# A planner that spaces the transfers that are not score shuffles evenly

## The chip, the cores and the metric

The kernel runs on one core of a Trainium2 chip, in one launch. The metric is the device time of that launch in microseconds (us); lower is better. The engines are TensorE (PE in the profile, with its weight loads as PEld), VectorE (DVE), ScalarE (ACT), GpSimd (POOL) and SyncE (SP), which here does nothing but issue DMA transfers. Sixteen DMA engines carry the transfers.

## What is computed

Two stages follow each other: attention whose heads are mixed before and after the softmax, and a feed-forward layer with a rational activation.

```python
B, H, S, D = 4, 12, 448, 64
scores = scale * q @ k.T                                  # (B, H, S, S)
scores = einsum('bhij,hg->bgij', scores, w_pre)           # mix the 12 heads
attn = exp(scores - max) ; attn /= sum(attn) + 1e-9
attn = einsum('bhij,hg->bgij', attn, w_post)              # mix them again
x = (attn @ v) as (B*S, H*D)                              # (1792, 768)
h = x @ w_in                                              # (1792, 2048)
P = a0 + a1*h + a2*h^2 + a3*h^3 ; Q = 1 + |b0|*|h| + |b1|*h^2
out = (P / (Q + 1e-6)) @ w_out                            # (1792, 768)
```

## The kernel before

**Attention** goes through 16 row tiles, T = 0 to 15, four to a batch. A tile has 120 query rows (88 in one tile of each batch). For each of six pairs of heads `put_qk` multiplies q with k on TensorE (line 496), VectorE or ScalarE copies the two score blocks from PSUM to a buffer `st` (lines 238 and 236; there are six such buffers), and one DMA for each head moves the copy into the tile `d` (line 512). This DMA is the **shuffle**: it brings the 12 heads of a row beside each other on the partitions, so that one matmul can mix them. A tile has 12 shuffles, and two tiles `d` are used in turn, so the shuffles of tile T can start only when the last mixing matmul of tile T-2 has read its `d`.

`put_pre` mixes the heads (line 565, `ps_t` or `ps_u` from `d`); its first group of a tile needs all 12 shuffles of that tile. The maximum (571), the exponential (580), the reciprocal (591) and the scaling of the second mixing weights (600) follow, then `put_post` (line 640), a transpose on VectorE (656) and `put_av` (line 705), which multiplies with v. The results go to a scratch tensor in DRAM (`x_scr`, line 728).

**The feed-forward layer** has 64 units: 18 matmuls with `w_in` (line 879), the rational function on ScalarE and VectorE, and 18 matmuls with `w_out` (line 969). The weights are 64-bit in DRAM; `put_w` loads a piece (`cr`, line 405), and ScalarE, VectorE and GpSimd turn it into two 32-bit halves. Three of the 16 blocks of weights are made during attention and stored in a scratch tensor (`w_scr`, line 449).

**The order of everything comes from a planner.** Each step is an `Op` with an engine, an assumed duration, the steps it depends on, an earliest time and a due time `at`. `Plan.run` plays this forward: at each moment it takes the engine that is free first, and of that engine's ready steps the one with the earliest due time. Transfers go through one model of the DMA queue: each `Op` on "sp" adds its `extra` to the time at which the queue is free, and SP may run at most `AHEAD` = 3 us ahead of it. The steps are then written out by their planned start, so each engine's instructions stand in that order. Nothing else of the plan reaches the chip: there every engine takes its own instructions one after the other, each as soon as the semaphores it waits for allow. A transfer that waits for nothing is issued right behind the one before it.

SP's transfers in attention are the shuffles and seven other kinds: q tiles (line 363, `q<-in_q`), pieces of k (375, `kk<-in_k`) and of v (679, `vv<-in_v`), the weight pieces (405, `cr<-in_w`), their stores (449, `w_scr<-co`), the stores of the attention result (728, `x_scr<-xs`), and a few constants. Most of them are made by `bulk`; the weight loads and stores call `add` themselves. `tau[g]` is the planned start of mixing group g, and `END1` the planned start of the feed-forward layer.

Of the kernel before, what the change touches and what calls it, by code (L numbers as in the profile page):

```python
# [37 lines left out]
CV = 384  # L38
# [3 lines left out]


class Op:
    __slots__ = ("eng", "dur", "fn", "deps", "at", "extra", "start", "end", "left", "behind", "since", "n", "on", "pick", "mode", "late")

    def __init__(self, eng, dur, fn, deps, at, extra, since, mode, late):
        self.late = late
        self.since, self.on, self.pick, self.mode = since, None, isinstance(eng, dict), mode
        self.eng, self.dur, self.fn, self.at, self.extra = eng, dur, fn, at, extra  # L50
        self.deps = deps
        self.start = self.end = None


class Plan:
# [6 lines left out]
    SLACK = 2.0  # L62

    def __init__(self):
        self.ops = []

    def add(self, eng, dur, fn, deps=(), at=0.0, extra=0.0, since=0.0, after=(), mode=None, late=0.0):
        op = Op(eng, dur, fn, [d for d in deps if d is not None], at, extra, since, mode, late)
        op.behind = list(after)
        self.ops.append(op)  # L70
        return op

    def run(self):
# [35 lines left out]
                ready(op)  # L109
        order = []  # L110
        last = None
        while True:
            if "sp" in free:
                free["sp"] = max(free["sp"], dma_free - self.AHEAD)
            best = None
            for e in todo:
                while todo[e] and todo[e][0][2].on:
                    heapq.heappop(todo[e])
                while wait[e] and wait[e][0][2].on:
                    heapq.heappop(wait[e])  # L120
                if todo[e]:
                    t = free[e]
                elif wait[e]:
                    t = max(free[e], wait[e][0][0])
                else:
                    continue
                if best is None or t < best[0]:
                    best = (t, e)
# [3 lines left out]
            while wait[e] and wait[e][0][0] <= t:  # L132
                _, n, op = heapq.heappop(wait[e])
                if op.on:
                    continue
                heapq.heappush(todo[e], (op.at, n, op))
            op = todo[e][0][2]
            if e == "pe" and op.mode != last:
                more = [x for x in todo[e] if not x[2].on and x[2].mode == last and x[0] <= op.at + self.SLACK]
                if more:  # L140
                    op = min(more)[2]
# [100 lines left out]
def mixed_attention_then_rational_ffn(ctx: ExitStack, tc, q, k, v, w, wmix, mask, a, b2, out):  # L242
# [8 lines left out]
    plan = Plan()  # L251
# [103 lines left out]

    def bulk(dur, fn, deps, at, nbytes, **more):

        return add("sp", dur, fn, deps, at=at, extra=dma(nbytes), **more)

    def put_q(T, at, since=0.0):  # L360
        def load():
# [37 lines left out]
    def put_w(f, c, at, since=0.0, g=None):  # L399
# [48 lines left out]
        def store():  # L448
            nc.sync.dma_start(out=w_scr[f][:, :, sl], in_=box["o"].bitcast(F32))

        ld = add("sp", 0.45, load, [R["cr"].take()], at=at - 5.0, extra=dma(128 * CV * 8), since=max(since, at - 9.0))
        near = lambda i, k: [] if g is None else [posts[min(g + i, len(groups) - 1)][k]]
        o1 = add("act", act(CV), mag, [ld, R["cm"].take(), *near(0, 3)], at=at, late=4.0)
        o2 = add({"dve": 0.32} if g is None else {"pool": 1.54}, 0, clamp, [o1, *near(0, 1)], at=at)
# [12 lines left out]
        o7 = add(subs(CV, on=ON["w_lo"]), 0, lo, [o6, *near(1, 1)], at=at)  # L467
        R["cm"].uses[-1].append(o7)
        if f in VIA:
            o8 = add("sp", 0.57, store, [o7], at=at, extra=dma(128 * CV * 8), late=2.0)  # L470
            R["co"].uses[-1].append(o8)
            w_done[f].append(o8)
        else:
            w_ld[f].append(o6)
            w_ld[f].append(o7)
# [578 lines left out]
    for u in range(len(units)):  # L1054
# [2 lines left out]
            put_w(i // NCV, i % NCV, at=END1 + UNIT * u + 2.0, since=END1 + UNIT * u - 6.0)  # L1057
        put_unit(u)

    with tc.manual_schedule():  # L1060
        for op in plan.run():
            if op.pick:
                op.fn({"act": nc.scalar, "dve": nc.vector, "pool": nc.gpsimd}[op.on])
            else:
                op.fn()
# [55 lines left out]
```

## Time and profile before

| | |
|---|---|
| time, median of 3 runs | 831.42 us (829.88 to 835.35) |
| the profiled execution: its own time, its span | 830.89 us, 829.1 us |
| TensorE busy | 801.0 us (97%) |
| VectorE, ScalarE, GpSimd busy | 690.6 (83%), 502.4 (61%), 222.2 (27%) |
| moved by DMA | 155.46 MB, 187 GB/s on average |
| TensorE's granted clock | 0.996 of full speed |

The span is the time from the first to the last instruction; 1.8 us of the execution lie around it. A busy TensorE is not a TensorE at its peak, because the ends of matmuls are modelled, so the page says less than the waits do. The granted clock is at its higher level (2.4 GHz) from the first 23 us on.

### The profile page before, as it was taken

The numbers are of one execution on the slowest core, as the hardware profiler recorded it, in microseconds if no ns is written. First come the engines' busy times: TensorE is split into PE (matmuls) and PEld (weight loads), VectorE is DVE, ScalarE is ACT, GpSimd is POOL, SyncE is SP. The second block draws the span as 40 slices with busy tenths as digits, with TensorE's granted clock in tenths as the row PEclk, the third lists the DMA queues.
The fourth block names the chain that finished last, engine by engine and source line by source line (L and its number), as shares of the span: only waits on it lengthen the run. The fifth ranks groups of instructions, "written<-read, shape, count | busy, mean of one in ns | idle before, by whom it ended". The sixth has DMA issues, their size and how long they took to land.

```text
span 829.1 us, 23254 instructions
## 1 busy us (share of the span) xinstructions
PE 801.0 (97%) x9360; PEld 598.0 (72%) x9360; DVE 690.6 (83%) x1252; ACT 502.4 (61%) x1099; POOL 222.2 (27%) x393
## 2 busy tenths in 40 slices
PE   5889999999999999999999999999999999999998
PEld 1244455554554445589999999999999999999997
DVE  5677788887888888888999998999889999677775
ACT  2456666655665566566776775677557677545632
POOL 2224444432444343721111212123212222100000
PEclk9999999999999999999999999999999999999999
DMA  6677878777887675985733255664477634466314
GB/s 201 207 214 224 246 259 265 222 202 231 260 259 212 217 235 171 335 276 210 256 125 101 81 207 133 215 141 104 88 228 192 165 82 67 78 225 231 122 57 156
DMA packets 71900, 155.46 MB, mean 187 GB/s; under 512 B 12560, under 2 KB 52336, under 8 KB 70640
## 3 DMA queue, kind: packets, MB, share of 16 engines
q1 hardware_dynamic: 67736, 141.99, 52.6%
q0 software_dynamic: 3456, 11.01, 8.2%
q8 instruction: 74, 1.21, 0.6%
q10 hardware_dynamic: 600, 0.97, 0.4%
q14 instruction: 34, 0.28, 0.1%
HBM read 77.49 MB, written 37.75 MB: 139 GB/s over the span
## 4 chain that ended last, share of the span: by engine, by line
PE 84%; DMA 6%; DVE 5%; ACT 2%; issue 1%; POOL 0%; SPq 0%; ACTq 0%; DVEq 0%; POOLq 0%
PE ps_s L879 28%; PE ps_u L969 9%; PE ps_t L969 9%; PE ps_a L969 9%; PE ps_s L496 8%; PE ps_a L640 7%; PE ps_t L565 4%; PE ps_u L565 4%; DMA d<-st 4%; PE ps_u L705 2%; PE ps_t L705 2%; DVE nm L571 2%; ACT e L580 2%; DMA kk<-in_k 1%; DVE aa L656 1%
## 5 line engine op out<-in xcount | busy, mean ns | idle before, releaser
L656 DVE STREAM_TRANSPOSE aa<-ps_a 128x448 f32<-128x448 f32 (+1 forms) x184 | 107.8, 618 | 11.6 <-PE ps_a L640 10.8
L879 PE MATMUL ps_s<-d,w 128*128 128x448 f32 x504 | 107.4, 366 | 0.0
L879 PE MATMUL ps_s<-xs,w 128*128 128x448 f32 x504 | 107.1, 366 | 0.0
L236 ACT COPY st<-ps_s 120x448 f32<-120x448 f32 (+1 forms) x120 | 60.4, 533 | 69.2 <-PE ps_s L496 38.3
L496 PE MATMUL ps_s<-kk,q 64*64 64x448 f32 x720 | 94.0, 552 | 8.3 <-DMA kk<-in_k 5.4
L446 POOL TENSOR_TENSOR w<-cm,w 128x384 fp32r<-128x384 f32 x48 | 53.7, 1118 | 177.8 <-ACT w L236 168.4
L600 POOL TENSOR_SCALAR krs<-kpost,rr 128x64 f32<-128x64 f32 x180 | 81.7, 468 | 72.1 <-DVE rr L591 51.3
L879 PEld LDWEIGHTS ps_s<-d,w 128*128 128x128 f32 x504 | 94.3, 188 | 8.7 <-issue 0.9
L879 PEld LDWEIGHTS ps_s<-xs,w 128*128 128x128 f32 x504 | 94.6, 188 | 7.9
L640 PEld LDWEIGHTS ps_a<-e,krs 64*32 64x32 f32 x2880 | 44.7, 106 | 74.4 <-issue 29.0
L640 PE MATMUL ps_a<-e,krs 64*32 64x224 f32 x2880 | 92.6, 355 | 1.6 <-DVE aa L656 0.8
L892 ACT ACTIVATE m<-ps_s,a_sb 128x448 f32<-128x448 f32 x64 | 46.2, 722 | 76.8 <-PE ps_s L879 73.4
L969 PE MATMUL ps_u<-g,w 128*128 128x448 f32 x336 | 84.1, 366 | 0.0
L969 PE MATMUL ps_a<-g,w 128*128 128x448 f32 x336 | 84.1, 366 | 0.0
L969 PE MATMUL ps_t<-g,w 128*128 128x448 f32 x336 | 83.9, 365 | 0.0
L580 ACT ACTIVATE e<-ps_t,nm 128x448 f32<-128x448 f32 x92 | 57.8, 635 | 25.4 <-DVE nm L571 17.1
L580 ACT ACTIVATE e<-ps_u,nm 128x448 f32<-128x448 f32 x88 | 55.3, 635 | 22.0 <-DVE nm L571 18.6
L969 PEld LDWEIGHTS ps_t<-g,w 128*128 128x128 f32 x336 | 63.1, 188 | 5.3
L969 PEld LDWEIGHTS ps_a<-g,w 128*128 128x128 f32 x336 | 63.1, 188 | 5.2
L969 PEld LDWEIGHTS ps_u<-g,w 128*128 128x128 f32 x336 | 63.1, 188 | 5.2
L496 PEld LDWEIGHTS ps_s<-kk,q 64*64 64x64 f32 x720 | 29.5, 135 | 49.4 <-issue 21.5
L915 ACT ACTIVATE ua<-sq 128x448 f32<-128x448 f32 x64 | 37.1, 580 | 33.6 <-DVE sq L912 33.4
(90 smaller groups left out, 1452.7 us busy)
## 6 DMA issues: line engine op xcount, KB each, us to landing
d<-st SPq DMA_DIRECT2D x144, 210.0 KB
cr<-in_w SPq DMA_DIRECT2D x64, 384.0 KB
d<-x_scr SPq DMA_DIRECT2D x5, 2688.0 KB
xs<-x_scr SPq DMA_DIRECT2D x4, 2688.0 KB
o_scr<-o POOLq DMA_DIRECT2D x24, 448.0 KB, 5.7
d<-st SPq DMA_DIRECT2D x42, 157.5 KB
x_scr<-xs SPq DMA_DIRECT2D x12, 540.0 KB
q<-in_q SPq DMA_DIRECT2D x16, 384.0 KB
```

What stands on the lines that cost most here:

```text
L236: eng.copy(o, i)
L446: eng.tensor_sub(t[:, 1, :], box["m"].bitcast(F32), t[:, 0, :].bitcast(F32))
L496: nc.tensor.matmul(box["s"][hh][i0:i1, 0:S], lhsT=Q[T][d, pr, i0:i1], rhs=K[b][d, pr, :], start=True, stop=True)
L565: nc.tensor.matmul(box[r if nt == 2 else 0]["t"][64 * c:64 * c + 64, 0:S], lhsT=kpre[p], rhs=Dt[T][p, kb + c if nt == 2 else kb, :], start ...
L580: nc.scalar.activation(e, box[r]["t"][:, 0:S], AF.Exp, bias=box[0]["nm"][:, r:r + 1], accum_out=box[0]["sm"][:, r:r + 1])
L600: eng.tensor_scalar_mul(box[r]["kr"], kpost, rr)
L640: nc.tensor.matmul(banks[c]["p"][q_:q_ + BT, JH * r:JH * (r + 1)], lhsT=box[r]["kr"][p, m_, :], rhs=box[r]["e"][p, JH * jh:JH * (jh + 1)], ...
L656: nc.vector.transpose(o, src)
L879: nc.tensor.matmul(h[:, 0:S], lhsT=W[fi][:, wi, kk * 128:(kk + 1) * 128], rhs=x[:, kk // 3, xj, kk % 3, :], start=(n == 0), stop=(n == 3 * ...
L892: nc.scalar.activation(new("m"), box["h"], AF.Identity, scale=a_sb[:, 3:4], bias=a_sb[:, 2:3])
L915: nc.scalar.activation(box["ua"], box["vv"], AF.Ln)
L969: nc.tensor.matmul(O[key][:, 0:S], lhsT=W[fi][:, wi, DM + m * 128:DM + (m + 1) * 128], rhs=box["g"][:, gi, :], start=(f == 0 and n == 0), ...
```

## The change

`Plan` gets a rule for SP. Steps made by `bulk` carry a mark, and the loads and stores of `put_w` are now made by `bulk` as well. When the planner has taken a marked step at time t, inside the stretch from `tau[2]` to `END1 - 24`, no other marked step may be taken before t + 2.4 us: those that are ready are put aside, and SP goes on with shuffles meanwhile. Shuffles and constants are not marked. Nothing is added to the program, and no transfer, matmul or vector operation changes its size; `at`, `since` and the assumed durations are the same.

```diff
     def run(self):
...
+        held = 0.0
+        aside = []
         while True:
             if "sp" in free:
                 free["sp"] = max(free["sp"], dma_free - self.AHEAD)
+                if aside and held <= free["sp"]:
+                    for x in aside:
+                        heapq.heappush(todo["sp"], x)
+                    aside = []
...
+            if e == "sp":
+                if aside and held <= t:
+                    for x in aside:
+                        heapq.heappush(todo[e], x)
+                    aside = []
+                while todo[e] and (todo[e][0][2].on or todo[e][0][2].gap and t < held):
+                    x = heapq.heappop(todo[e])
+                    if not x[2].on:
+                        aside.append(x)
+                if not todo[e]:
+                    continue
             op = todo[e][0][2]
+            if op.gap and self.spaced[0] <= t < self.spaced[1]:
+                held = t + self.gap
...
     def bulk(dur, fn, deps, at, nbytes, **more):
-        return add("sp", dur, fn, deps, at=at, extra=dma(nbytes), **more)
+        op = add("sp", dur, fn, deps, at=at, extra=dma(nbytes), **more)
+        op.gap = True
+        return op
...
-        ld = add("sp", 0.45, load, [R["cr"].take()], at=at - 5.0, extra=dma(128 * CV * 8), since=max(since, at - 9.0))
+        ld = bulk(0.45, load, [R["cr"].take()], at=at - 5.0, nbytes=128 * CV * 8, since=max(since, at - 9.0))
...
+    plan.spaced, plan.gap = (tau[2], END1 - 24.0), 2.4
```

TensorE's instructions stand in exactly the order they had. SP's order in attention changes in many places; VectorE's, ScalarE's and GpSimd's change in three short pieces of attention and then through most of the feed-forward layer.

SP, the transfers behind the last shuffles of tile 1 (the `x12` row) and among the first shuffles of tile 2. Before:

```order
L512 DMA d<-st 10x12x448 x12
L363 DMA q<-in_q 128x768
L679 DMA vv<-in_v 128x768 x3
L512 DMA d<-st 10x12x448 x2
L679 DMA vv<-in_v 128x384
L512 DMA d<-st 10x12x448 x4
L363 DMA q<-in_q 128x768
```

Now (lines are counted 25 further down in the changed file):

```order
L537 DMA d<-st 10x12x448 x12
L388 DMA q<-in_q 128x768
L704 DMA vv<-in_v 128x768 x2
L537 DMA d<-st 10x12x448 x2
L704 DMA vv<-in_v 128x768
L537 DMA d<-st 10x12x448 x2
L704 DMA vv<-in_v 128x384
L537 DMA d<-st 10x12x448 x2
L388 DMA q<-in_q 128x768
```

The third and the fourth piece of v each moved behind two more shuffles of tile 2.

SP, from the end of tile 7 (shuffles `10x9x448`) through tile 8 (`10x12x448`). Before:

```order
L679 DMA vv<-in_v 128x768
L512 DMA d<-st 10x9x448 x2
L363 DMA q<-in_q 128x768
L405 DMA cr<-in_w 128x768
L679 DMA vv<-in_v 128x768
L512 DMA d<-st 10x12x448 x2
L449 DMA w_scr_119<-co 256x1x384
L512 DMA d<-st 10x12x448 x4
L679 DMA vv<-in_v 128x768
L512 DMA d<-st 10x12x448 x6
L679 DMA vv<-in_v 128x384
```

Now:

```order
L400 DMA kk<-in_k 128x448
L704 DMA vv<-in_v 128x768
L388 DMA q<-in_q 128x768
L537 DMA d<-st 10x12x448
L704 DMA vv<-in_v 128x768
L537 DMA d<-st 10x12x448 x2
L474 DMA w_scr_119<-co 256x1x384
L537 DMA d<-st 10x12x448 x3
L430 DMA cr<-in_w 128x768
L537 DMA d<-st 10x12x448 x2
L704 DMA vv<-in_v 128x768
L537 DMA d<-st 10x12x448 x4
```

Two transfers stood between the first and the last shuffle of tile 8, and four do now.

VectorE in the feed-forward layer, about a quarter of the way through, around the split of an activation into its halves (`g`). Before:

```order
L929 SCALAR_TENSOR_TENSOR ua<-m,a_sb,ua 128x448
L238 CAST g<-ua 128x448
L939 TENSOR_TENSOR g<-ua,g 128x448
L238 COPY o<-ps_t 128x448
L905 TENSOR_TENSOR m<-m,ps_s 128x448
```

Now:

```order
L954 SCALAR_TENSOR_TENSOR ua<-m,a_sb,ua 128x448
L440 TENSOR_SCALAR cm<-cm 128x384
L444 TENSOR_SCALAR cm<-cm 128x384
L964 TENSOR_TENSOR g<-ua,g 128x448
L449 SCALAR_TENSOR_TENSOR cg<-cr,cm 128x384
L455 SCALAR_TENSOR_TENSOR cm<-cr,cg 128x384
L261 COPY o<-ps_t 128x448
```

The cast went to ScalarE, and a weight piece moved ahead. In the whole layer VectorE had 32 of the 64 casts and has 20 now; of the 72 copies of results (`o`) it had 38 and has 42.

Counted from SP's order for each tile: the transfers that are no shuffles between the last shuffle of the tile before and the first of this one ("gap"), and between this tile's first and last shuffle ("inside").

| tile | 2 | 3 | 4 | 5 | 6 | 7 | 8 | 9 | 10 | 11 | 12 | 13 | 14 | 15 |
|---|---|---|---|---|---|---|---|---|---|---|---|---|---|---|
| gap before | 4 | 2 | 3 | 5 | 5 | 5 | 3 | 2 | 5 | 6 | 2 | 1 | 4 | 2 |
| gap now | 3 | 2 | 3 | 3 | 3 | 2 | 3 | 3 | 3 | 3 | 3 | 2 | 3 | 2 |
| inside before | 4 | 6 | 3 | 2 | 5 | 3 | 2 | 4 | 5 | 4 | 3 | 3 | 4 | 2 |
| inside now | 5 | 6 | 3 | 4 | 5 | 6 | 4 | 3 | 6 | 5 | 4 | 4 | 4 | 2 |

Tiles 0 and 1 have none, apart from the first loads.

## Rows read from the trace of the kernel before

**Rows 1.** Stretches: us, busy (instructions) by engine, granted clock, DMA share, GB/s.

```profile
0.00:23.00 23.00, 14.40 (x84) 4.85 (x88) 11.11 (x14) 4.99 (x8) 5.50 (x8) 0.88 0.61 201
23.00:347.00 324.00, 308.50 (x6656) 154.46 (x6652) 263.24 (x485) 198.29 (x533) 135.12 (x302) 1.00 0.76 234
347.00:824.60 477.60, 477.60 (x2632) 438.53 (x2624) 415.08 (x753) 299.11 (x560) 81.61 (x84) 1.00 0.53 156
824.60:829.10 4.50, 0.54 (x3) 0.16 (x1) 1.20 (x2) 0.00 (x0) 0.00 (x0) 1.00 0.42 153
```

**Rows 2.** TensorE's timeline, first mixing group of tiles 1, 2, 4, 6, 8, 9.

```profile
36.74 0.98 PE L565 MATMUL ps_t<-d,kpre 64*64 64x448 f32 x8 [1.92 <-DMA vv<-in_v]
...
60.36 0.98 PE L565 MATMUL ps_u<-d,kpre 64*64 64x448 f32 x8 [1.02 <-DMA kk<-in_k]
...
103.38 0.98 PE L565 MATMUL ps_u<-d,kpre 64*64 64x448 f32 x8 [0.73 <-DVE nm L571]
...
144.97 0.98 PE L565 MATMUL ps_u<-d,kpre 64*64 64x448 f32 x8 [0.43 <-DVE nm L571]
...
187.22 1.25 PE L565 MATMUL ps_t<-d,kpre 64*64 64x448 f32 x8 [1.40 <-DMA d<-st]
...
208.30 0.98 PE L565 MATMUL ps_u<-d,kpre 64*64 64x448 f32 x8 [0.39 <-DVE nm L571]
```

**Rows 3.** The chain that ended last, its DMA pieces: start, us to landing.

```profile
46.83 7.26 DMA d<-st
...
54.11 6.23 DMA kk<-in_k
...
170.25 6.88 DMA d<-st
```

**Rows 4.** Waits on VectorE, 23 to 345 us: total, times, longest.

```profile
DVE st L238 <- DMA d<-st: 3.0, 5, 1.0
```

**Rows 5.** DMA issues: count, KB each.

```profile
d<-st SPq DMA_DIRECT2D x144, 210.0 KB
...
vv<-in_v SPq DMA_DIRECT2D x12, 384.0 KB
```

**Rows 6.** Short stretches, columns as in the first group.

```profile
36.00:38.00 2.00, 1.25 (x16) 0.57 (x16) 0.34 (x3) 0.00 (x0) 0.46 (x1) 1.00 1.01 391
38.50:40.50 2.00, 1.40 (x16) 0.45 (x21) 0.38 (x1) 1.98 (x5) 0.00 (x0) 1.00 0.05 19
...
97.00:103.00 6.00, 5.57 (x140) 2.99 (x136) 4.67 (x9) 3.20 (x9) 2.01 (x6) 1.00 0.99 285
...
165.00:167.00 2.00, 2.00 (x40) 0.88 (x24) 2.00 (x4) 1.84 (x6) 0.72 (x2) 1.00 0.30 97
176.50:179.50 3.00, 2.82 (x77) 1.68 (x76) 2.25 (x5) 0.12 (x2) 0.55 (x2) 1.00 0.65 227
```

**Rows 7.** SP's timeline, 23 to 62 us: start, us in which it issued.

```profile
22.96 7.72 SPq L512 DMA_DIRECT2D d<-st  x7
30.73 0.49 SPq L363 DMA_DIRECT2D q<-in_q  x1
31.28 2.02 SPq L679 DMA_DIRECT2D vv<-in_v  x3
39.08 1.65 SPq L512 DMA_DIRECT2D d<-st  x2
40.78 0.49 SPq L679 DMA_DIRECT2D vv<-in_v  x1
```

**Rows 8.** TensorE's timeline, the first product with v.

```profile
46.15 1.34 PE L705 MATMUL ps_u<-aa,vv 64*64 64x90 f32 x56
```

**Rows 9.** First part of the feed-forward layer, columns as in the first group.

```profile
420.00:570.00 150.00, 150.00 (x740) 138.63 (x740) 143.29 (x261) 102.09 (x194) 29.74 (x29) 1.00 0.48 140
```

**Rows 10.** Groups of instructions: the casts on VectorE, busy us, mean ns.

```profile
L238 DVE CAST g<-ua 128x448 fp32r<-128x448 f32 x32 | 18.1, 566 | 3.4 <-PE ps_a L969 1.4
```

More of the change, by code (lines that the diff above doesn't have):

```diff
@@ L44 @@
 class Op:
-    __slots__ = ("eng", "dur", "fn", "deps", "at", "extra", "start", "end", "left", "behind", "since", "n", "on", "pick", "mode", "late")
+    __slots__ = ("eng", "dur", "fn", "deps", "at", "extra", "start", "end", "left", "behind", "since", "n", "on", "pick", "mode", "late", "gap")
     def __init__(self, eng, dur, fn, deps, at, extra, since, mode, late):
-        self.late = late
+        self.late, self.gap = late, False
         self.since, self.on, self.pick, self.mode = since, None, isinstance(eng, dict), mode
@@ L64, in __init__ @@
     def __init__(self):
-        self.ops = []
+        self.ops, self.spaced, self.gap = [], (0.0, 0.0), 0.0
     def add(self, eng, dur, fn, deps=(), at=0.0, extra=0.0, since=0.0, after=(), mode=None, late=0.0):
@@ L124, in run @@
                     t = max(free[e], wait[e][0][0])
+                    if e == "sp" and aside and held < t:
+                        t = held
+                elif e == "sp" and aside:
+                    t = held
                 else:
@@ L469, in put_w @@
         if f in VIA:
-            o8 = add("sp", 0.57, store, [o7], at=at, extra=dma(128 * CV * 8), late=2.0)
+            o8 = bulk(0.57, store, [o7], at=at, nbytes=128 * CV * 8, late=2.0)
             R["co"].uses[-1].append(o8)
```

## Prediction

> **What bounds the kernel now.** I read the busy time by stage first. From 347.0 to 824.6 us TensorE is busy in all 477.60 us of 477.60 at the full clock [rows 1]: the feed-forward layer is TensorE's own matmuls back to back, and no order of transfers makes it shorter. What can be won lies in attention. From 23 to 347 us TensorE is busy for 308.50 of 324.00 us [rows 1], so 15.5 us are idle there. The first 23 us lie before the planner's spacing begins.
>
> Next I read where TensorE idles. The largest pieces stand ahead of the first mixing group of a tile: 1.92, 1.02, 0.73, 0.43, 1.40 and 0.39 us for tiles 1, 2, 4, 6, 8 and 9 [rows 2], together 5.89 us. Of what ended these waits the trace names three times a DMA and three times the maximum on VectorE. The names are those of whatever came last on a semaphore, so they need reading: the mixing matmul reads neither v nor k, but it does need all 12 shuffles of its tile. The chain shows the kind of delay: a shuffle issued at 46.83 took 7.26 us to land, one at 170.25 took 6.88 us, and the piece ahead of tile 2 lasts 6.23 us [rows 3]. I take all six waits as waits for a tile's last shuffle; for the three that name the maximum this is an inference. One more effect of late shuffles shows: VectorE's copies wait 3.0 us in five places for a buffer `st` to come free [rows 4].
>
> Last I read how fast transfers run. In a stretch of shuffles alone the DMA engines are busy by 0.65 at 227 GB/s [rows 6]; a shuffle of 210 KB [rows 5] thus takes 215,040 / 227,000 = 0.95 us. With loads of v alone the share is 1.01 at 391 GB/s, so a piece of 384 KB takes 393,216 / 391,000 = 1.0 us. I use 1.0 us for each transfer that is no shuffle. Twelve shuffles are 11.4 us and some seven others 7 us: a tile of about 21 us (from 187.22 to 208.30 [rows 2]) has little DMA time to spare, and between full stretches there are holes: a share of 0.05 from 38.5 to 40.5 us and 0.30 from 165 to 167 us [rows 6]. In these holes nothing is left to move, because the next tile's shuffles aren't ready.
>
> **The change part by part.** The plan's 2.4 us don't reach the chip; only the order does. SP issues what waits for nothing at once: q and three pieces of v went out from 30.73 to 33.30 us, and SP then stood at the next shuffle until 39.08 [rows 7]. So each moved transfer is priced by the shuffles it now stands behind, and by the hole that it leaves.
>
> (1) *Tile 1.* Its last shuffles are issued by 30.68 us [rows 7], and q and two pieces of v still stand right behind them. The 1.92 us stay: 0, with bounds of -0.5 and 0.
>
> (2) *Tile 2.* The third piece of v ran while nothing else had to (391 GB/s from 36 to 38 us), just ahead of the hole. Now it is issued after two shuffles of tile 2, at about 40.8 us, where the fourth piece was [rows 7]. The hole gets 1.0 us larger, and the full stretch behind it has 1.0 us more to move before tile 2's last shuffle lands, which TensorE awaits at 60.36 us: **+1.0 us**, bounds 0 and +2. The fourth piece of v now goes out after two more shuffles, some 2.4 us later, near 43.1. The product with v at 46.15 us [rows 8] needs that piece for its last seventh; by the transfers ahead of it, it lands near 48 us, an estimate from 0.95 us a shuffle and from the 3 to 7 us that transfers take to land here. TensorE may wait about 1 us there. That wait lies ahead of the one at 60.36 on the same engine, which then shrinks by as much, so it is not added.
>
> (3) *Tiles 3 to 5.* Tile 3 keeps its numbers. Tile 4 keeps them too, with one piece of v two shuffles earlier; the transfers ahead of the last shuffle are the same: 0 on its 0.73 us, bounds -0.7 and 0. Tile 5 has two fewer in the gap and two more inside. The gap before it is full (0.99 from 97 to 103 us [rows 6]), so what leaves it is made up inside, and tile 5's start shows no wait: 0.
>
> (4) *Tile 6.* By the table, two transfers fewer stand ahead of its last shuffle: its 0.43 us go. **-0.43 us.** A tile of one or two fewer (10 to 12) shows no wait in the rows at which this could count.
>
> (5) *Tiles 7 and 8.* Three leave the gap before tile 7 and three enter it; tile 7's start shows no wait that this could lengthen at once. Tile 8 has two transfers more inside. Its shuffles start after the hole from 165 to 167 us, so a queue that is emptier before them doesn't help. The bounds are 0 (the two run where a shuffle is late anyway) and +2.0 us (two at 1.0 us, all on the path to the 1.40 us wait). I take **+1.0 us**, as for tile 2, the nearest place with a row: the same hole, one transfer with its whole price.
>
> (6) *Tile 9.* One fewer inside, one more in the gap: the 0.39 us go. **-0.39 us.**
>
> (7) *Copies that wait for `st`.* The 3.0 us [rows 4] are VectorE's, and TensorE sees a part of them. Spaced transfers stand behind a pair of shuffles instead of in a run: some waits shrink and others grow. I take 0, bounds -3 and +2.
>
> (8) *The feed-forward layer.* TensorE's order is the same, and its idle time is 0. VectorE is busy for 143.29 of 150 us in the first part [rows 9], and it loses 12 casts of 0.566 us [rows 10] and gains four copies of about the same length: some 4.5 us less over the layer. ScalarE is at 102.09 of 150 and covers what it takes over. 0; if this cover failed, each late activation would stop TensorE, which is a rival below.
>
> The sum: +1.0 - 0.43 + 1.0 - 0.39 = +1.18 us. The profiled execution took 830.89 us, which gives **832.1 us**. The median of the three runs is 0.53 us above that execution; the forecast is worth the same on either within the runs' scatter. About 1%, 8.3 us, is what a measurement of this kernel can tell from no change.
>
> A rule of the Trainium skill bears on this (DMA: Bandwidth & Descriptors, Rules for kernel authors): to overlap a transfer with compute, issue it early and wait for it late. It speaks against the change, which issues v later at tile 2. The trace agrees as far as the hole at 38.5 us goes: v loaded there cost nothing. By the rule taken alone, parts (2) and (5) would come in at their upper bounds, and the sum would be +3.2 us.
>
> **The rivals.**
>
> *Faster: the last shuffle meets fewer neighbours.* If the 6 to 7 us that a shuffle takes to land [rows 3] come from runs of four or five transfers issued together, an even mix lets each shuffle through, and most of the 5.89 us of tile starts go, with some of the copies' waits on top: about -5, 826 us. For it: the longest wait, 1.92 us, stands right beside the run of q and v. Against it: that run hardly changes, and transfers that only swap places before the last shuffle of a tile take the same time in total. It decides if the queue is idle for less time than now between tiles.
>
> *Slower: the gaps run dry.* Twelve transfers more stand inside tiles (2, 5, 7, 8, 10 to 13) and one fewer in tile 9. They leave gaps in which shuffles can't run and enter stretches in which shuffles have to. At 1.0 us each that is 12 us if all of it came to lie on the path: 843 us. Half of it, where tiles are within half a microsecond of waiting now, gives +6, 837 us. It decides when the DMA share in the gaps before tiles 5, 7 and 11 falls under a half. Against it: tiles 5, 7 and 10 to 13 show no large wait now and have some slack.
>
> *No change: the order doesn't matter.* The shuffles alone keep the DMA engines busy by only 0.65 [rows 6], as if some engines never had a part in them; those that do are then full through nearly all of attention, and time follows the sum of their work, which isn't changed: 830.9 us. The Trainium skill states a cause (DMA: Bandwidth & Descriptors, Why a DMA increments its semaphore by 16 and not by 1): a transfer whose slowest dimension is 10 runs on the ten lowest engines. Ten of 16 is 0.63, and the 0.65 of the trace agrees. This is also the case in which the change doesn't do what it says, since the even spacing exists in the plan alone.
>
> *Slower in the second stage.* A cast that waits its turn on ScalarE makes an activation late, and TensorE stops: with 44 casts there, a loss of 0.1 us at each (an assumed size; no row shows one) would be 4.4 us, 835 us. VectorE's lighter load speaks against it.
>
> **How the numbers follow.** Chances: the forecast 0.35, no change 0.20 (within 1.2 us of it), the even mix 0.22, dry gaps 0.17, the second stage 0.06. The range goes from 825.5, just under the even mix, to 837.5, just over half of the dry gaps; I leave about 1 in 10 on either side. Faster by over 1% (under about 823) needs all the tile waits and half of the copies' as well: 0.05. Slower by over 1% (over about 840) needs most of the dry gaps: 0.08. Within 1%: 0.87.
>
> **What would show it right or wrong.** In the profile after: the wait ahead of tile 2's first mixing group near 2 us, or a wait inside the first product with v; tile 8's above 1.40; those of tiles 6 and 9 gone; a DMA share still near 0.76 from 23 to 347 us; no idle TensorE in the feed-forward layer. I would be wrong if the idle time of attention fell to 10 us or less (even mix), if holes appeared in the gaps before tiles 5, 7 and 11 (dry gaps), or if TensorE waited at line 969 or 879.

## The result, and the profile after

The kernel after took 841.68 us (median of 4 executions, 840.68 to 844.46), the kernel before 832.98 us (4 executions, 829.88 to 835.35): a ratio of 1.0112, 95% interval 1.0066 to 1.0158. In a second comparison it took 840.51 us (6 executions) against 832.54 (17), a ratio of 1.0102 (1.0067 to 1.0137). The change makes the kernel slower by about 1%, 8 to 9 us. The prediction had 832.1 us and a range up to 837.5; both missed it.

The profiled execution took 844.46 us with a span of 842.7, so it is 13.6 us longer than the profiled one of before, though the medians differ by 8.7. Both kernels scatter by some 5 us within these comparisons (the kernel before from 828.05 to 839.87 us over all of them), and these two profiles come from opposite ends: the one is the longest of its four, the other among the shortest. What a trace shows once may be chance; a place counts below only where it comes again.

Busy time by stage of the kernel after (columns: stretch, its length, busy time of PE, PEld, DVE, ACT, POOL with the number of instructions, granted clock, DMA share, GB/s), to be read beside [rows 1]:

```profile
23.00:360.60 337.60, 313.84 (x6664) 155.65 (x6660) 264.22 (x487) 196.90 (x530) 134.60 (x302) 0.99 0.74 224
360.60:838.20 477.60, 477.60 (x2631) 438.65 (x2624) 414.26 (x745) 303.32 (x569) 82.31 (x84) 1.00 0.53 156
```

The feed-forward layer is the same: 477.60 us, all busy. Attention is 13.6 us longer and TensorE idles 23.8 us in it (337.60 - 313.84), not 15.5. The mean granted clock is 0.99 where it was 1.00.

So of the 13.6 us, 8.3 are more idle time and 5.3 are more busy time for the same work. About half of the idle time has a name that the prediction didn't count. TensorE's waits in attention that end in "issue", which means that the trace shows nothing that they waited for (line: total, times, longest), first before, then after:

```profile
PE ps_u L705 <- issue: 1.6, 2, 0.9
PE ps_t L705 <- issue: 1.3, 1, 1.3
```

```profile
PE ps_u L730 <- issue: 3.4, 2, 1.8
PE ps_t L730 <- issue: 2.0, 1, 2.0
PE ps_a L665 <- issue: 1.5, 1, 1.5
```

That is 2.9 us before and 6.9 us after. What they are is read further down, at tile 13. Most of the extra busy time are two stretches of about 3.4 us at half clock, from 151.9 and from 302.1 us: work that takes 3.4 us there takes 1.7 us at the full clock.

The clock has a share in the medians too. Every run lists its mean granted clock: 0.9912 on the mean of the ten runs of the kernel after and 0.9933 on that of the 97 of the kernel before. The difference of 0.0021 times a span of 840 us gives 1.8 us of the 8 to 9, an estimate that takes TensorE as busy throughout.

TensorE's timeline at the first mixing groups of tiles 2, 5, 6 and 8 in the kernel after (start, length, engine and line, operation, in brackets the idle time before it and what the trace names as its end), beside [rows 2]:

```profile
62.15 0.61 PE L590 MATMUL ps_u<-d,kpre 64*64 64x448 f32 x4 [1.57 <-DVE aa L681]
...
127.79 0.61 PE L590 MATMUL ps_t<-d,kpre 64*64 64x448 f32 x4 [0.87 <-DMA w_scr<-co]
...
151.16 0.61 PE L590 MATMUL ps_u<-d,kpre 64*64 64x448 f32 x4 [2.77 <-DVE xs L748]
...
197.90 0.59 PE L590 MATMUL ps_t<-d,kpre 64*64 64x448 f32 x2 [2.71 <-DMA q<-in_q]
```

So tile 2 waits 1.57 us (before 1.02), tile 6 2.77 (0.43) and tile 8 2.71 (1.40), and tile 5, which did not wait, waits 0.87.

The chain of waits of the kernel after, ahead of tile 8 (start, length, what):

```profile
181.79 7.27 DMA d<-st
...
189.07 8.84 DMA q<-in_q
```

The mixing group reads no q. As in the prediction, the wait is taken as one for the tile's last shuffles, which were issued from 184.61 to 187.95 us; that is an inference.

And SP's timeline there, of the kernel after and then of the kernel before (length is the time from the first issue of the run to the end of its last):

```profile
173.01 0.79 SPq L537 DMA_DIRECT2D d<-st  x1
173.84 0.49 SPq L704 DMA_DIRECT2D vv<-in_v  x1
174.44 1.96 SPq L537 DMA_DIRECT2D d<-st  x2
176.49 0.57 SPq L474 DMA_DIRECT2D w_scr<-co  x1
177.16 3.97 SPq L537 DMA_DIRECT2D d<-st  x3
181.17 0.51 SPq L430 DMA_DIRECT2D cr<-in_w  x1
181.79 1.75 SPq L537 DMA_DIRECT2D d<-st  x2
183.59 0.93 SPq L704 DMA_DIRECT2D vv<-in_v  x1
184.61 3.34 SPq L537 DMA_DIRECT2D d<-st  x4
```

```profile
165.25 1.65 SPq L512 DMA_DIRECT2D d<-st  x2
166.99 0.57 SPq L449 DMA_DIRECT2D w_scr<-co  x1
167.66 3.54 SPq L512 DMA_DIRECT2D d<-st  x4
171.25 0.91 SPq L679 DMA_DIRECT2D vv<-in_v  x1
172.26 6.40 SPq L512 DMA_DIRECT2D d<-st  x6
```

Four transfers stand among the twelve shuffles of tile 8 and not two, and two of the four stand in its second half. That is what a moved transfer looks like on the chip.

Tile 6 is another matter. The instructions on the tile `xs` in the kernel after, 145 to 152 us (what they sat idle for, and who waited for them):

```profile
its engine sat idle before it (us, times) until:
  DMA x_scr<-xs: 0.5, 1
...
who waited for it (us, times):
  PE ps_u L590: 2.8, 1
```

There is one buffer `xs`. ScalarE may write the next batch's result into it only when the stores of the batch before have read it, and TensorE needs the bank `ps_u` that this frees. The stores are marked transfers. The last pair of batch 0 on SP in the kernel before, then the last one in the kernel after (where tile 5 already starts 3.9 us later):

```profile
129.60 1.02 SPq L728 DMA_DIRECT2D x_scr<-xs  x2
```

```profile
143.22 1.36 SPq L753 DMA_DIRECT2D x_scr<-xs  x1
```

On the chip only 0.5 us of TensorE's 2.77 are a wait of ScalarE for a store. The planner knows of the late stores too, and in its order the cast now stands behind a copy of scores and an exponential. ScalarE's timeline at the cast, first before, then after:

```profile
141.85 0.82 ACT L236 CAST xs<-ps_u 128x360 fp32r<-128x360 f32 x2
```

```profile
147.57 0.53 ACT L259 COPY st<-ps_s 90x448 f32<-90x448 f32 x1 [1.88 <-issue]
148.00 0.63 ACT L605 ACTIVATE e<-ps_t,nm 128x448 f32<-128x448 f32 x1
...
149.23 0.82 ACT L259 CAST xs<-ps_u 128x360 fp32r<-128x360 f32 x2 [0.51 <-DMA x_scr<-xs]
```

The product that the cast reads ended at 141.77 us before and at 145.63 after, so the cast came 0.1 us behind it and comes 3.6 us behind it now. In the second execution of the kernel after ScalarE doesn't wait for a store at all, and TensorE still waits 2.23 us.

What follows the wait costs as well. Stretches of 1 us of the kernel after (columns as above):

```profile
148.00:149.00 1.00, 0.39 (x19) 0.00 (x0) 0.92 (x2) 0.72 (x3) 0.00 (x0) 1.00 0.13 39
...
150.00:151.00 1.00, 0.00 (x0) 0.00 (x0) 0.91 (x2) 0.68 (x3) 0.22 (x1) 1.00 0.71 245
151.00:152.00 1.00, 0.84 (x9) 0.47 (x13) 0.19 (x2) 0.00 (x0) 0.65 (x2) 0.95 0.97 279
152.00:153.00 1.00, 1.00 (x12) 0.28 (x4) 0.70 (x1) 0.00 (x0) 0.21 (x1) 0.50 0.84 240
...
154.00:155.00 1.00, 1.00 (x32) 0.44 (x16) 0.44 (x1) 1.00 (x4) 0.00 (x0) 0.50 0.02 8
```

TensorE stood from 148.4 to 151.2 us, and just after it started again its granted clock fell to 0.50, the lower level of 1.2 GHz, for over 3 us.

The time from one tile's first mixing group to the next tile's is the measure that the experiments share. It is the difference of two starts like those above; each is of one profiled execution. "2" is the way from tile 1 to tile 2.

| kernel | 2 | 4 | 5 | 6 | 7 | 8 | 13 |
|---|---|---|---|---|---|---|---|
| before | 23.62 | 21.72 | 20.55 | 21.04 | 21.27 | 20.98 | 20.86 |
| after | 25.69 | 22.75 | 21.98 | 23.37 | 23.16 | 23.58 | 23.00 |
| after, again | 25.95 | 21.06 | 23.14 | 22.83 | 23.17 | 22.27 | 24.40 |
| queue only | 25.78 | 22.32 | 21.99 | 22.61 | 22.48 | 22.11 | 23.66 |
| engines only | 24.77 | 20.92 | 20.54 | 24.28 | 23.18 | 19.03 | 20.58 |
| no x | 25.24 | 22.61 | 21.03 | 21.16 | 21.29 | 19.88 | 21.63 |
| only x | 24.86 | 21.59 | 20.55 | 20.53 | 21.28 | 21.28 | 21.02 |
| only v | 25.62 | 20.91 | 20.53 | 21.41 | 21.28 | 18.83 | 21.89 |
| no x, no v | 24.54 | 21.06 | 20.87 | 21.95 | 22.41 | 23.31 | 20.60 |
| no w | 25.98 | 20.93 | 21.38 | 22.72 | 21.28 | 21.50 | 20.86 |
| gap 2.0 | 27.54 | 20.92 | 20.55 | 22.16 | 21.79 | 21.91 | 20.61 |
| gap 2.8 | 24.62 | 22.45 | 22.69 | 23.76 | 22.80 | 23.89 | 22.58 |
| tiles 2, 4, 5 mended | 25.11 | 23.74 | 22.12 | 23.07 | 22.91 | 21.47 | 21.51 |
| tiles 6, 8 mended | 25.64 | 22.44 | 21.71 | 22.50 | 21.46 | 20.47 | 22.90 |
| all five mended | 24.21 | 22.57 | 20.54 | 21.40 | 21.88 | 19.95 | 21.78 |
| tails free | 23.07 | 20.91 | 20.54 | 21.57 | 21.27 | 19.37 | 20.67 |
| tails free, again | 23.37 | 20.93 | 20.78 | 21.22 | 21.27 | 18.79 | 21.30 |

After against before these seven columns add up to +13.5 us, as much as the whole difference; what the columns left out gain and lose nearly cancels (-1.1 us to tile 1, +0.6 to 9, +0.9 to 12, -0.8 to 14). The same kernel twice ("after" and "after, again") differs by up to 1.7 us in one column, so a single figure says little below that. Some kernels also lose in columns left out: no w takes 26.50 and 25.09 us to tiles 10 and 11, no x and no v 25.12 us to tile 11, and before these are 21.41 and 21.62.

### The profile page after: what moved, and what is told of

The parts are those of the page before. It is cut to its first block, busy times and chain, and to the rows that moved or that the text cites. A ratio compares the mean times of both kernels' runs of the same rounds, so it can differ in the third digit from the quotient of the medians.

```text
span 842.7 us, 23271 instructions
## 1 busy us (share of the span) xinstructions
PE 805.5 (96%) x9360; PEld 598.6 (71%) x9360; DVE 690.8 (82%) x1246; ACT 505.2 (60%) x1105; POOL 222.4 (26%) x393
## 4 chain that ended last, share of the span: by engine, by line
PE 73%; DVE 4%; DMA 2%; ACT 2%; issue 1%; POOL 0%; ACTq 0%; POOLq 0%; DVEq 0%
PE ps_s L904 28%; PE ps_u L994 9%; PE ps_t L994 9%; PE ps_a L994 9%; PE ps_a L665 4%; PE ps_s L521 4%; PE ps_u L590 2%; PE ps_t L590 2%; PE ps_u L730 2%; PE ps_t L730 2%; ACT e L605 1%; DMA d<-st 1%; DVE nm L596 1%; DMA q<-in_q 1%; DVE aa L681 1%
## 5 line engine op out<-in xcount | busy, mean ns | idle before, releaser
L521 PE MATMUL ps_s<-kk,q 64*64 64x448 f32 x720 | 98.1, 565 | 9.5 <-DMA kk<-in_k 5.2
L596 DVE TENSOR_REDUCE nm<-ps_t 128x2 f32<-128x896 f32 (+1 forms) x47 | 49.7, 1057 | 9.8 <-PE ps_t L590 8.1
```

Of the source, the lines that this page charges most:

```text
L521: nc.tensor.matmul(box["s"][hh][i0:i1, 0:S], lhsT=Q[T][d, pr, i0:i1], rhs=K[b][d, pr, :], start=True, stop=True)
L596: nc.vector.tensor_reduce(out=nm[:, 0:nt], in_=box[0]["both"][:, 0:nt, 0:S], axis=AX.X, op=ALU.max, negate=True)
```

## The experiments

Five explanations were on trial. A: shuffles land late because more transfers stand ahead of a tile's last one. B: the loss is in the order of VectorE, ScalarE and GpSimd, which the new plan changes too. C: the late stores of `xs`. D: the line of marked transfers is too full, so the least urgent are pushed far back. E: each kind of transfer has its own price.

**Queue and engines apart.** The planner is run twice, and each engine's order is taken from one of the two plans:

```diff
+    def merge(self, compute, queue):
+        for part, gap in ((False, compute), (True, queue)):
+            for op in self.sched(todo, gap):
+                if (op.on == "sp") == part:
+                    lines.setdefault(op.on, []).append((op.start, op.n, op, op.on))
...
-        for op in plan.run():
+        for op in plan.merge(0.0, 2.4):    # the second kernel: plan.merge(2.4, 0.0)
```

> The change comes apart into the order of SP's transfers and the order in which VectorE, ScalarE and GpSimd do their work. This kernel has SP's order of the kernel after and the three engines' order (and choice of engine) of the kernel before. Theory A, the queue: the shuffles that now stand behind moved transfers land later, and that alone makes most of the 8.7 us between the medians: 838 to 843 us, starts of tiles 2, 4, 5 and 8 as late as in the kernel after. Theory B, the engines' order: the loss is made where VectorE's subtractions of xs moved behind other work (TensorE waits 2.8 us for one ahead of tile 6), and the queue's order alone costs about the +1.2 us of the prediction: 832 to 835 us, with no wait for xs ahead of tile 6.

> The other half: SP's order of the kernel before, the three engines' order and choice of engine of the kernel after. Theory A, the queue: within 2 us of the kernel before (831 to 835 us). Theory B, the engines' order: 838 to 843 us, and the wait of some 2.8 us for xs ahead of tile 6 is there again. If both halves cost 3 to 6 us, the loss is shared.

Queue only: 839.68 us against 834.17, ratio 1.0088 (1.0054 to 1.0122). Engines only: 839.49, ratio 1.0076 (1.0049 to 1.0102). Neither theory has it alone. The halves add up to 1.0164, more than the change as a whole, though the intervals nearly meet. In the table, the queue alone makes the losses of tiles 2, 4, 5, 8 and 13. Tile 6 is lost by either half: with the queue's order alone the cast comes 2.8 us behind its product and TensorE waits 2.0 us; with the engines' order alone the stores are early (the last one at 128.3 us), but the cast keeps its late place, VectorE's subtraction of `xs` stands behind two transposes, and TensorE waits 2.2 us. So that loss is counted in both halves. The engines alone also lose at tile 7, where the clock is low behind the wait, and wait 3.0 us in the feed-forward layer, which the kernel after doesn't; that may come from joining two plans that don't fit, but it wasn't tried.

**One kind at a time.** The mark is set or taken away behind the step:

```diff
                     x_st.setdefault(b, []).append(s_)
+                    s_.gap = False      # no x
...
             v_ld[b].append(bulk(
+            v_ld[b][-1].gap = False     # no v
...
-        op.gap = True                   # only x, only v: the one kind is marked again behind it
```

> All of the change, but the stores of xs are not spaced. In the kernel after the last store of batch 0 is issued at 143.2 us (before: 130.2) and ScalarE's cast of the next batch into the one buffer xs has to wait for it; TensorE then stands 2.8 us ahead of tile 6 and its clock falls to 0.50 for about 3.5 us. Theory C, the stores: with them unmarked that wait and the low clock behind it are gone and 4 to 5 us come back: 836 to 838 us. Theory A, late shuffles alone: tile 6 starts as late as in the kernel after, 839 to 843 us.

> Only the stores of xs are spaced, all else is as in the kernel before. Theory C: the cast of batch 1 waits again, TensorE stands about 2 to 3 us ahead of tile 6, with or without the low clock behind it: 836 to 839 us. Theory A: 832 to 835 us, like the kernel before, since no transfer comes to stand before a shuffle that is late.

> Only the pieces of v are spaced. It tests the term of +1.0 us for tile 2 and the cover of the first product with v. By the prediction's own terms: 833 to 835 us, tile 2's first mixing group 1 us later than before (60.4 us), and a wait of about 1 us in the first product with v. Theory C: the same here, since no store of xs is moved; no wait ahead of tile 6.

> The change without the stores of xs and without v: q, k, the loads of w and the stores of split w are spaced; the order of VectorE, ScalarE and GpSimd stands as in the kernel before but for one swap. Theory C with the price of v: both causes are gone, within 2 us of the kernel before. Theory A, every transfer moved in between shuffles costs 1.0 us: seven or so of the twelve are still moved, 838 to 841 us.

Against a kernel before of 831.95 us: no x 836.57, ratio 1.0061 (1.0037 to 1.0086); only x 832.26, 1.0000 (0.9975 to 1.0025); only v 832.82, 1.0028 (1.0000 to 1.0056); no x and no v 833.13, 1.0019 (0.9995 to 1.0044). Without the mark on the stores, tiles 6 and 7 are back at 21.16 and 21.29 us, as theory C has it: the cast follows its product at once again (0.1 us). But only half of the loss comes back. Spaced alone, the stores cost nothing: the last one is then issued at 134.8 us, early enough for the cast. Theory C names a true wait that needs the other transfers to come about. With only v spaced, tile 2's first mixing group starts at 61.60 us, 1.2 us later than before, about what was forecast there, though its total isn't clear of the noise. No x and no v stays within 2 us of the kernel before, as theory C with the price of v has it.

**How full the line is.**

```diff
         ld = bulk(0.45, load, [R["cr"].take()], at=at - 5.0, nbytes=128 * CV * 8, since=max(since, at - 9.0))
+        ld.gap = False       # no w
...
             o8 = bulk(0.57, store, [o7], at=at, nbytes=128 * CV * 8, late=2.0)
+            o8.gap = False       # no w
...
-    plan.spaced, plan.gap = (tau[2], END1 - 24.0), 2.4
+    plan.spaced, plan.gap = (tau[2], END1 - 24.0), 2.0    # and 2.8
```

> q, k, v and the stores of xs are spaced by 2.4 us, the loads of w and the stores of split w are not. VectorE's and GpSimd's orders are those of the kernel before, ScalarE's but for two rows. Theory D, the crowd: the stores of xs and v come late in the full change because too many marked transfers share one line (some 96 in 297 us, one per 3.1 us on the mean, and more than one per 2.4 us around tiles 4 to 6); with the 21 of w out of the line the last store of batch 0 goes out after 74 shuffles and not after 78, nothing waits for it at tile 6, and the time is 832 to 835 us. Theory E, each kind has a price of its own: spaced x and v cost here what they cost in the full change, 838 to 841 us.

> All of the change with a gap of 2.0 us. VectorE's and GpSimd's orders come out as in the kernel before; 93 rows of SP's order still differ. Theory D: the line is shorter, the last store of xs of batch 0 goes out after 74 shuffles, no wait for it at tile 6: 833 to 836 us, mostly the price of v at tile 2 (1.1 us). Theory A, late shuffles at 1.0 us each: the same transfers stand inside tiles, 838 to 842 us.

> All of the change with a gap of 2.8 us. Theory D: the line is longer, the stores of xs wait at least as long as at 2.4 (the last two after 78 shuffles), v and q come later too, and the time is over that of the kernel after by 3 us or more: 844 to 855 us. Theory A: the number of transfers inside tiles grows little, 840 to 845 us.

Against 833.31 us: no w 837.71, ratio 1.0044 (1.0015 to 1.0074); gap 2.0 us 840.45, 1.0106 (1.0046 to 1.0166); gap 2.8 us 850.55, 1.0215 (1.0160 to 1.0271). No w lies between the two theories. At 2.8 us theory D is right: the cost doubles. At 2.0 it is wrong about the total. The stores are in time there, and no wait for `xs` shows at tile 6, but the kernel is as slow as at 2.4. Its one profiled execution lost the time as theory A has it, at tile 2. TensorE's waits of that kernel from 40 to 70 us (line, waited for: total, times, longest), and its stretches at the end of that wait:

```profile
PE ps_u L590 <- DMA d<-st: 3.3, 1, 3.3
```

```profile
63.00:64.00 1.00, 0.00 (x0) 0.00 (x0) 0.00 (x0) 0.00 (x0) 0.01 (x1) 0.77 0.59 182
64.00:65.00 1.00, 0.65 (x4) 0.33 (x8) 0.00 (x0) 0.00 (x0) 0.00 (x0) 0.50 0.91 260
```

A wait for the last shuffle of 3.3 us, and half the clock from 63.5 us on, before the wait is over: the way to tile 3 then took 23.74 us instead of 21.30.

**Single places undone.** In the queue-only kernel SP's order is set back in some tiles, with all else held. A letter is a transfer: s a shuffle, V v, K k, Q q, c a load of w, w a store of split w, X a store of `xs`.

```diff
+        for r, want in {2: "QVVVssVssssQssKssKss", 4: "cwVssQssVssssssVss", 5: "cwVQXssssXssssXssss"}.items():
+            rows_[r] = [by[k].pop(0) for k in want]
...
+        for r, want in {6: "XKwssXXcssXXssQssssss", 8: "KVQsVsswssssssssscV"}.items():
```

The queue-only kernel has "QVVssVssVssQssKssKss", "cwVssQssVssssVssss", "cwVssQssXssXssXssss" in the first three, "XKwsscssXssQssXssXss" (and one more X behind) and "KVQsVsswssscssVssss" in the other two.

> The first experiment's kernel (the full change on SP's queue, the other engines as before), with SP's order in tiles 2, 4 and 5 as in the kernel before: the same transfers, v and the stores in their old places among the same twelve shuffles. From one tile's first mixing group to the next that kernel took 25.78 us to tile 2, 22.32 to tile 4 and 21.99 to tile 5, the kernel before 23.62, 21.72 and 20.55. Theory A, the place of a transfer ahead of a tile's last shuffle sets the tile's start: these three come back to within 0.5 us of the kernel before, some 3 us together less a part that shows elsewhere, 836 to 838 us. Theory C, only the stores of xs count: no change at these tiles, 838 to 841 us.

> The first experiment's kernel with two other places undone: the last five stores of xs of batch 0 go out before the ninth shuffle of tile 6 instead of up to 84 shuffles in, and in tile 8 the last load of w and the last piece of v stand behind the twelfth shuffle. That kernel took 22.61 us to tile 6, 22.48 to tile 7 and 22.11 to tile 8; the kernel before 21.04, 21.27 and 20.98. Theory C for tiles 6 and 7, theory A for tile 8: no wait for xs ahead of tile 6 (2.0 us there), 6 and 7 together 2 us shorter, tile 8 about 1 us shorter: 836 to 838 us. If the stores are not the cause, tile 6 keeps its wait.

> Both mendings in one kernel, tiles 2, 4, 5, 6 and 8; the other ten tiles keep the spaced order. If these places are the whole loss on the queue's side: within 2 us of the kernel before (832 to 836 us). If the spacing costs everywhere a little: 837 to 840 us.

Against 833.49 us: tiles 2, 4, 5 mended 842.12, ratio 1.0109 (1.0073 to 1.0144); tiles 6, 8 mended 841.01, 1.0112 (1.0074 to 1.0150); all five 837.10, 1.0064 (1.0035 to 1.0093). Against the queue-only kernel's 1.0088 (1.0054 to 1.0122) none of the three moved the total beyond the noise, and the first two missed the 836 to 838 us that were expected. All five together came to 837.10 us, inside the 837 to 840 given for a spacing that costs everywhere a little; it is lower than the other two at the edge of the noise. The places themselves answer more clearly. With the stores early, the wait for `xs` is gone; the instructions on `xs` around tile 6, first with tiles 2, 4, 5 mended (stores late), then with tiles 6, 8 mended (stores early):

```profile
its engine sat idle before it (us, times) until:
...
  DMA x_scr<-xs: 3.3, 1
```

```profile
its engine sat idle before it (us, times) until:
  ACT xs L312: 0.2, 1
```

Tiles 6 and 7 together take 43.96 us there, and 43.28 with all five mended, against 45.09 (queue only) and 45.98 (stores late); that is 1.1 us where 2 were expected, and the kernel before has 42.31. Tile 8 takes 20.47 and 19.95 against 22.11 and 21.47. Tile 5 is back at 20.54 with all five mended. In the 22.12 with tiles 2, 4, 5 mended there is no wait either, but a stretch of about 3.4 us at half clock from 107.6 us on. Tile 4 isn't mended by its old order (23.74 and 22.57), and the traces say why: the old order has a wait ahead of its first mixing group (1.96 and 1.15 us here, 0.73 in the kernel before), and the spaced order has none. What tile 4 loses with the spaced order are stands by the name of issue inside it, 1.53 us in the kernel after and 0.47 in queue only; in the second execution of the kernel after they are missing, and tile 4 takes 21.06 us.

**The reverse on the kernel before.** Pieces of k and v among the last four shuffles of a tile go behind its last shuffle:

```diff
+            elif 0 < left <= 4 and name(x) in ('put_k', 'put_v'):
+                late.append(x)
```

> The reverse test on the kernel before: the pieces of k and v that stand among the last four shuffles of a tile (two in tile 2, one each in tiles 3, 4, 7 and 11) go out behind its last shuffle. Theory A at 1.0 us for each: tiles 2 and 4 start 1 and 0.7 us earlier, 830 to 832 us against a kernel before of 832 to 834 us. If the transfers run beside the shuffles for nothing, no change.

> The version with free tails once more. If the gain is real, a ratio between 0.994 and 0.999 again; if it was chance, an interval around 1.

830.54 us against 833.49, ratio 0.9970 (0.9941 to 0.9999), and the second time 830.53 against 832.54, 0.9991 (0.9962 to 1.0020). Its tiles 2 and 4 took 23.07 and 20.91 us, then 23.37 and 20.93, as theory A says, but a gain of 1 to 3 us in 832 is at the edge of what can be measured; it isn't shown to be faster than the kernel before.

**The kernel after once more.**

> The kernel after, unchanged, once more. What belongs to the order of transfers comes again: from one tile's first mixing group to the next 25.3 to 26 us to tile 2, 22.2 to 22.8 to tile 4, 21.5 to 22.2 to tile 5, a wait of 2 to 3 us for xs ahead of tile 6, 21.5 us or more to tile 8. What belongs to the one execution may be missing: the stretch at half clock near 300 us, and the longest instruction wait. 838 to 844 us.

840.51 us, ratio 1.0102 (1.0067 to 1.0137). What comes again: tile 2 (25.95 us), tiles 4 and 5 together (44.20; after 44.73, before 42.27), though each missed its range, tile 4 below it and tile 5 above, the late cast of `xs` ahead of tile 6 and the low clock behind it (46.00 for tiles 6 and 7 together; after 46.53, before 42.31), tile 8 (22.27), and tile 13 (24.40), which had been taken for chance.

Tile 13 is TensorE's own wait. It stops inside a group of matmuls that has all its data. The timeline of the kernel after, and its DMA queues from 299.5 to 299.6 us (queue and kind: packets, MB, share of 16 engines):

```profile
298.55 1.34 PE L730 MATMUL ps_t<-aa,vv 64*64 64x90 f32 x53
301.90 0.29 PE L730 MATMUL ps_t<-aa,vv 64*64 64x90 f32 x2 [2.00 <-issue]
```

```profile
q8 instruction: 1, 0.02, 54.9%
```

One packet of instructions moves at 299.5 us, 0.95 us after the group began, and TensorE goes on 2.4 us later. In the kernel before the packet moves at 286.4, 0.2 us after the group began, and TensorE goes on at 288.92, 2.5 us later, after 1.33 us of standing:

```profile
286.23 1.36 PE L705 MATMUL ps_t<-aa,vv 64*64 64x90 f32 x55
288.92 0.29 PE L705 MATMUL ps_t<-aa,vv 64*64 64x90 f32 x1 [1.33 <-issue]
```

Queue only: 1.25 us after the group began and 2.5 us to the restart; after, again: 2.3 and 2.3, with 3.22 us of standing. Fifteen of the seventeen traces have a stand at this place, and in all of them TensorE goes on 2.3 to 2.5 us after such a packet began. Over attention they show 57 stands of more than 0.4 us by the name of issue, 53 of them with a packet 2.2 to 3.1 us ahead of the restart. So the wait is as long as the instructions are late. In these three executions with SP's whole spaced order they come later than in the kernel before, but with only v spaced they come as late as in the kernel after (2.15 us of standing); by what, was not tried.

The stand is not all that tile 13 lost. In the three executions with SP's whole spaced order the clock falls to half around its end, and with only v spaced it doesn't. One stretch of the kernel after:

```profile
303.00:304.00 1.00, 1.00 (x11) 0.44 (x7) 0.95 (x4) 0.01 (x1) 0.28 (x1) 0.50 1.01 315
```

Only v takes 21.89 us to tile 13 with a stand of 2.15 us, the kernel after 23.00 with one of 2.00 us. The longer stand (0.7 us more than before, 1.9 in the second execution) and the 1.7 us of half clock make 2.4 and 3.6 us, and the table has +2.1 and +3.5.

## Why the prediction was wrong

The forecast of +1.18 us fell. None of the rivals is right as it stood either; nearest is "the gaps run dry", with the right size (837 to 843 us) and at tiles 2, 5 and 8 about its price of 1.0 us for a transfer inside, but without its sign in the gaps (below) and without a wait in tile 7, where three transfers more stand inside.

- *Tile 1, 0:* the order didn't change, but the 1.92 us that were to stay are the largest wait there of all seventeen traces (0.26 to 1.45 in the others, 0.83 and 0.48 in the kernel after). Tile 1 thus came 1.1 us earlier, which makes the way to tile 2 look longer by as much.
- *Tile 2, +1.0 us:* right. Eight kernels with v in this spaced order took 24.62 to 25.98 us (mean 25.57), six with the old order 23.62 to 25.11 (mean 24.52): +1.0; the 27.54 of the 2.0 us gap, where v stands in yet another order, is not among them. The wait in the first product with v came too (1.2 us in the kernel after) and was rightly not added.
- *Tiles 3 to 5, 0:* this step failed at tile 5. It waits 0.87 and 1.79 us ahead of its first mixing group and takes +1.4 and +2.6 us. "What leaves it is made up inside, and tile 5's start shows no wait: 0" took a tile without a wait for one with slack; it had none to spare, and two transfers more inside it cost their price at once. At tile 4 the step was right: its wait of 0.73 us is gone, and the +1.0 us of the one execution are a stand for instructions that the other doesn't have.
- *Tile 6, -0.43 us:* this step failed most. Only transfers ahead of shuffles were counted. Nobody was asked who waits for a *store*: the last stores of `xs` went from 129.60 to 143.22 us, and the cast, the bank and TensorE hang on them, either by the wait on the chip (queue only) or by the place that the planner then gives the cast (engines only); without the mark on the stores both are gone. Tile 6 lost 2.3 and 1.8 us.
- *The clock* had no term. A wait that is followed by half clock costs more than its own length: tile 7 took 23.16 and 23.17 us behind such waits and 21.27 without, +1.9.
- *Waits for instructions* had no term either. They grew from 2.9 to 6.9 us in the two traces, and with the clock behind them they make tile 13's +2.1 and +3.5 us.
- *Tile 8, +1.0 us, up to +2.0:* right in cause, since the wait ahead of it is gone once the two transfers stand behind its shuffles; its size was +2.6 and +1.3. The wait is 2.71 us in one execution and 1.33 in the other (before 1.40), and 0.7 us of waiting for `st` inside the tile come on top in both. *Tile 9, -0.39:* the wait went, but its way got no shorter (21.69 us for 21.08), because a stand for instructions inside it grew from 0.76 to 1.81 us.
- *Copies, 0; feed-forward layer, 0:* the second is right (477.60 us busy of 477.60). TensorE's waits for `st` went from 1.5 to 2.4 us in the two traces, well within the bounds of the first.

The deciding sign of the dry gaps, a DMA share under a half, did not come. The stretches of 6 us before tiles 5, 7 and 11 in the kernel after:

```profile
99.00:105.00 6.00, 4.47 (x112) 2.60 (x104) 2.78 (x6) 2.16 (x6) 1.81 (x5) 1.00 0.84 241
142.00:148.00 6.00, 5.89 (x148) 3.26 (x148) 4.70 (x10) 2.28 (x6) 3.12 (x6) 1.00 0.69 215
235.00:241.00 6.00, 5.94 (x152) 3.17 (x144) 3.91 (x8) 2.73 (x8) 1.94 (x5) 1.00 0.86 253
```

0.84, 0.69 and 0.86; in the kernel before, the gaps ahead of tiles 5 and 7 had 0.99 [rows 6] and 0.87, so they did become emptier, but not by as much as the rival asked. "No change" fell with the total. What stays open: the share of each place in the median (the single places don't add up to it), why the instructions come later, and why some waits are followed by half clock and others not.

## What to carry to other kernels

Before a queue's order is changed, list for each transfer who waits for its end: of a load the reader, of a store whoever wants its source buffer back. A planner that knows of a late transfer also moves the work behind it, so an order that looks like another engine's can have its cause in the queue. A tile that shows no wait need not have slack; look at how long its last input lands before its use. And price a wait of TensorE with what its clock does afterwards, which the rows right behind similar waits show.

## What the runs showed of the hardware

TensorE's granted clock fell from 1.00 to 0.50 just after it went on from a wait of 2.77 us (kernel after, tile 6), and stayed there while TensorE was busy all the time, from 152 to 155 us; with a gap of 2.0 us it fell inside the wait of 3.3 us ahead of tile 2. The length of a wait doesn't settle it in these traces: it also fell at a stand of 2.00 us (kernel after, tile 13), and it stayed at 1.00 after waits of 2.95 us (engines only, at 60.68 us) and 3.40 us (no x and no v, at 255.49 us). TensorE also waits for its own instructions: at one place in fifteen traces it went on 2.3 to 2.5 us after a packet of the instruction queue had begun to move. The Trainium skill (Runtime: NRT & Kernel Launch, Instruction fetch mechanics) says that each engine fetches blocks of instructions by its own DMA queue and that crossing a block is mostly hidden; the queue agrees with these traces, and so does "mostly" in the kernel before, where it stands for over 0.4 us behind 3 of the 52 packets that begin from 23 to 347 us; the hiding doesn't hold at this place, with 1.33 us of standing before and 2.00 and 3.22 after.
